# Moving x pairs to other PSUM banks, re-ordering query sums, and adding a third block of x on GpSimd in a fused attention and highway kernel

## The chip, the cores and the metric

The kernel runs on one core of one Trainium2 chip. Times are device microseconds (us) of that core. A kernel's time is the median of its runs; a profile is one execution, whose span is some 2 us shorter than the time of its run. The granted clock is the share of TensorE's full clock that the profile shows it was given.

Medians and ranges below are of all runs. A run over 1.5% above the fastest of its kernel counts as slow and is left out of the ratios, which are the mean time of one kernel's fast runs over that of the other's fast runs of the same rounds. The base of a ratio matters here: those of e1 to e3 come out at 133.45 us for the kernel before and those of e6 to e8 at 133.07, while all its fast runs on these chips average 132.62 and 132.28.

The engines are TensorE (PE), VectorE (DVE), ScalarE (ACT), GpSimd (POOL) and the queue that starts transfers (SP). In the timelines here each one's instructions follow the order in which the program issues them, and it waits where an input or a buffer is not ready.

## The reference, cut to what matters

```python
def _attn_ref(q, k, v):                      # 8 batches, 8 heads, 576 rows, 64 wide
    q_s = exp(q - max(q)); q_s = q_s / sum(q_s, axis=-1)
    k_s = exp(k - max(k)); k_s = k_s / sum(k_s, axis=2)
    kv = einsum('bhsd,bhse->bhde', k_s, v)
    return einsum('bhsd,bhde->bhse', q_s, kv)

def _moe_ref(x, w_h, w_t, b_t):              # x: 4608 x 512, from the attention
    H = maximum(x @ w_h, 0)
    T = 1 / (1 + exp(-(x @ w_t + b_t)))
    return T * H + (1 - T) * x               # = T * (H - x) + x
```

For each batch the kernel makes kv, then x, then the gates T and H. The last form of the result is the one it uses: g = T * (H - x) from DVE, plus x. That last plus x is what the third part of the change moves.

## The kernel before

The kernel's steps are placed by hand: `at(p, step)` puts a step at position p, and steps are issued in order of p, eight positions to a batch. So p decides what stands before what in each engine's queue. `E(f, ...)` only delays the call.

```python
    ps_ht = pool("ps_ht", 4, space=PSUM)     # the gates' banks
    ps_2 = pool("ps_2", 1, space=PSUM)       # one tile of two banks
    ps_1 = pool("ps_1", 1, space=PSUM)
    ps_nat = pool("ps_nat", 1, space=PSUM)
    # ... (cut)
    def x_pair(b, a, how, left=False, singles=False):
        # ... (cut: four x products; banks are two of ps_ht if singles, else the two of ps_2)
        copy = {"A": nc.scalar.copy, "V": nc.vector.tensor_copy}
        # ... (cut: "AV" copies the first bank on ACT and the second on DVE, "A" both on ACT)

    added = lambda g: (0, 1) if g < 3 else (0, 1, 2)

    def add_x(c, ob):                        # g += x for block ob of batch c, on GpSimd
        xv, gv = views(c)
        nc.gpsimd.tensor_add(gv(ob), gv(ob), xv(ob))

    def turn_block(t, k_, xs, us):           # transpose on PE; adds x there if xs is given
        dst = t[:, k_, :]
        if xs is not None:
            mm(dst, xs, ident, True, False)
        mm(dst, us, ident, xs is None, True)
    # ... (cut)
    # in out_tile(g, n): four blocks of the pair of batches 2g and 2g+1
            turn_block(t, k_,
                None if k_ in added(g) else xT[g][:, k_, n].rearrange("p b d -> p (b d)"),
                gT[g][:, k_, n].rearrange("p b d -> p (b d)"))
    # ... (cut)
    # placing, for pair g: the eight output tiles; and for chunk (batch) c the adds
            for i in range(8):
                at(16 * (g + 1) + 2 + 2 * i, E(out_tile, g, i))
    for c in range(2, B):
        for ob in added(c // 2):
            at(8 * c + 2 * ob + 2.5, E(add_x, c, ob))
    # placing, for batch b with p = 8 * (b - 1): exp of the queries, half sums, scale
            e0, e1, s0, s1, sc = {
                3: (-2.6, -1.6, -1.1, -0.1, 1),
                4: (-5.5, -4.5, -3.7, -2.7, -2.6),
            }.get(b, (-5, -4, -3.9, -2.9, -2.8))
            # ...
            at(p + s0, E(q_sums, b, 0))
            at(p + s1, E(q_sums, b, 1), E(q_recip, b))
            at(p + sc, E(q_scale_p, b, 0, 4), E(q_scale_p, b, 4, N9))   # on GpSimd
            s = p + {3: 0, 4: 0}.get(b, -0.5)
            at(s, E(exp_half, b, "k", 0), E(cast_v, b, 0))              # cast on GpSimd
            at(s + 0.9, E(cast_v, b, 1))
```

The softmax here doesn't subtract the row's maximum and nothing guards it: scores larger than these inputs give would overflow.

Of the kernel before, what the change touches and what calls it, by code (L numbers as in the profile page):

```python
# [9 lines left out]
FP32 = mybir.dt.float32  # L10
# [8 lines left out]
def kernel(  # L19
# [10 lines left out]
    nc = tc.nc  # L30
    B, H, S, D = q.shape
    P = 128
# [17 lines left out]
    eqp = pool("eqp", 2)  # L50
    small = pool("small", 2)
    qtp = pool("qtp", 2)
    xtp = pool("xtp", 3)
    gp = pool("gp", 2)
    mo = pool("mo", 3)
    ps_ht = pool("ps_ht", 4, space=PSUM)
# [102 lines left out]
    def two_banks(name, dt=FP32):  # L159
        return ps_2.tile([P, 2, 2048 // (4 if dt is FP32 else 2)], dt, tag="q2", name=name)  # L160

    single = lambda name: ps_1.tile([P, 512], FP32, tag="q1", name=name)
    nat_bank = lambda name, dt=FP32: ps_nat.tile(
        [P, 512 if dt is FP32 else 1024], dt, tag="nat", name=name
# [114 lines left out]
    def x_mm(dst, b, a, c, x, n0, n1):  # L279
        r = slice(64 * c, 64 * c + 64)  # L280
        mm(
            dst[64 * x : 64 * x + 64], kvn[b % 2][r, x, a, :],
            qsT[b][r, 2 * a + x, n0:n1, :].rearrange("p n d -> p (n d)"), True, True,
        )


    def x9_mm(t, b, c):
        for a in range(2):
            for x in range(2):
                x_mm(t[:, c, a, :], b, a, c, x, NM, N9)  # L290

    def x9_copy(b, t, c=slice(0, 2)):
        x9v = x9.rearrange("p (a c) b d -> p c a b d", c=2)
        nc.vector.tensor_copy(x9v[:, c, :, b, :], t)

    def x_left(b):
        for c in range(2):
            name = f"px_{b}_l{c}"
            t = single(name) if c == 0 else two_banks(name)[:, 0] if b == 1 else nat_bank(name)
            t = t[:, 0:128].rearrange("p (z a w) -> p z a w", z=1, a=2)  # L300
            for a in range(2):
                for x in range(2):
                    x_mm(t[:, 0, a, :], b, a, c, x, NM, N9)
            x9_copy(b, t, slice(c, c + 1))
# [2 lines left out]



    def x_pair(b, a, how, left=False, singles=False):  # L310
        g, b2 = b // 2, b % 2
        if a == 0 and b2 == 0:
            xT[g] = xtp.tile([P, 4, NM, 2, 64], FP16, tag="xT", name=f"xT_{g}")
        if left and a == 0:
            t9 = ps_1.tile([P, 512], FP32, tag="q1", name=f"px_{b}_l")
            x9t[b] = t9[:, 0:256].rearrange("p (c a w) -> p c a w", c=2, a=2)
        if singles:
            t = [
                ps_ht.tile([P, 512], FP32, tag="ht", name=f"px_{b}_{a}_{c}")
                for c in range(2)  # L320
            ]
        else:
            t2 = two_banks(f"px_{b}_{a}")
            t = [t2[:, c] for c in range(2)]
        if left and a == 0:
            x9_mm(x9t[b], b, 0)
        for c in range(2):
            for x in range(2):
                x_mm(t[c], b, a, c, x, 0, NM)
        if left and a == 1:  # L330
            x9_mm(x9t[b], b, 1)
        dst = xT[g][:, 2 * a : 2 * a + 2, :, b2, :]
        view = lambda t: t.rearrange("p (n d) -> p n d", d=64)
        copy = {"A": nc.scalar.copy, "V": nc.vector.tensor_copy}
        if len(how) == 1:
            copy[how](dst, t2.rearrange("p c (n d) -> p c n d", d=64))  # L336
        else:
            for c in range(2):
                copy[how[c]](dst[:, c], view(t[c]))  # L339
        if left and a == 1:  # L340
            x9_copy(b, x9t[b])
# [51 lines left out]
        )  # L393


    added = lambda g: (0, 1) if g < 3 else (0, 1, 2)

    def add_x(c, ob):
        xv, gv = views(c)
# [82 lines left out]
    def at(p, *fs):  # L482
        events.setdefault(p, []).extend(fs)

    E = lambda f, *a: (lambda: f(*a))

    for c in range(1, B + 2):
        for ob in range(4):
            p = 8 * c + 2 * ob
# [6 lines left out]
    for g in range(B // 2):  # L496
        p = 16 * (g + 1)
# [6 lines left out]
    p = 8 * B + 8  # L504
# [1 line left out]
    at(p + 4, E(tile9, 1, 4))  # L506
    at(p + 8, E(tile9, 2, 3), E(tile9, 3, 3), E(last9))

    at(8, E(cast_v_head, 2, 0, nc.gpsimd), E(q_scale_p, 2, 0, 4), E(q_scale_p, 2, 4, 8))
    at(8.2, E(x_left, 1))  # L510
    at(9, E(exp_half, 2, "k", 0))
    at(10, E(cast_v_head, 2, 1, nc.scalar), E(exp_half, 2, "k", 1))
    at(10.5, E(blend, 0, 3))
# [7 lines left out]
    for b in range(2, B):  # L521
        p = 8 * (b - 1)
        if b > 2:
            e0, e1, s0, s1, sc = {
                3: (-2.6, -1.6, -1.1, -0.1, 1),
                4: (-5.5, -4.5, -3.7, -2.7, -2.6),
            }.get(b, (-5, -4, -3.9, -2.9, -2.8))
            at(p + e0, E(exp_half, b, "q", 0))
            at(p + e1, E(exp_half, b, "q", 1))
            at(p + s0, E(q_sums, b, 0))  # L530
            at(p + s1, E(q_sums, b, 1), E(q_recip, b))
            at(p + sc, E(q_scale_p, b, 0, 4), E(q_scale_p, b, 4, N9))
            s = p + {3: 0, 4: 0}.get(b, -0.5)
            at(s, E(exp_half, b, "k", 0), E(cast_v, b, 0))
            at(s + 0.9, E(cast_v, b, 1))
            at(s + 1, E(exp_half, b, "k", 1))
        tr, kv, x = {
            2: ((5, 6, 6.9), (4, 6.2), (7, 7.5)),
            3: ((3.5, 4.9, 5.1), (4, 4), (5.9, 6.9)),
            4: ((2, 3, 4), (4.5, 4.5), (5.9, 6.9)),  # L540
        }.get(b, ((2, 3, 4), (4, 4), (5, 6)))
        for i in range(3):
            at(p + tr[i], E(q_trans, b, i))
        at(p + kv[0], E(kv_half, b, 0))
        at(p + kv[1], E(kv_half, b, 1), E(kv_norm, b))
        at(p + x[0], E(x_pair, b, 0, "A", b > 2))
        at(p + x[1], E(x_pair, b, 1, "AV" if b == 2 else "A", b > 2, b == 2))
        if b == 2:
            at(p + 7.6, E(x_left, 2))
    for b in range(4, B):  # L550
        at(8 * (b - 3), *[E(load, b, w) for w in "qkv"])

    for f in [
        E(warm_up, 24),
        E(exp_half, 0, "q", 0), E(q_sums, 0, 0),
        E(exp_half, 0, "q", 1), E(q_sums, 0, 1),
        E(q_recip, 0), E(q_scale_v, 0, 0, 4), E(q_scale_v, 0, 4, N9),
        E(exp_half, 0, "k", 0), E(cast_v, 0, 0),
        E(exp_half, 0, "k", 1), E(cast_v, 0, 1),
        E(q_trans, 0, 0), E(q_trans, 0, 1, lambda: two_banks("pq_0_1", FP16)[:, 0]), E(warm_up, 2), E(q_trans, 0, 2, lambda: nat_bank("pq_0_2", FP16)),  # L560
        E(warm_up, 6),
        E(kv_half, 0, 0), E(gate_bias), E(warm_up, 2), E(kv_half, 0, 1), E(kv_norm, 0),
        *[E(cast_weight, "t", k_, (nc.vector, nc.gpsimd)[k_ % 2]) for k_ in range(4)],
        E(warm_up, 4),
        E(x_pair, 0, 0, "AA"), E(warm_up, 2), E(x_pair, 0, 1, "AV", False, True), E(warm_up, 1), E(x_left, 0),
        E(exp_half, 1, "q", 0), E(q_sums_tree, 1, 0),
        E(exp_half, 1, "q", 1), E(q_sums_tree, 1, 1), E(q_recip, 1),
        *[f for k_ in range(4) for f in (E(less_one, k_), E(cast_weight, "h", k_, nc.scalar, 0.5))],
        E(q_scale_p, 1, 0, 4), E(q_scale_p, 1, 4, 8),
        E(gate, 0, 0), E(gate, 0, 1), E(gate, 0, 2, lambda: two_banks("pt_0_2")[:, 0]), E(warm_mid, 5),  # L570
        E(carry, 0, 0), E(blend, 0, 0), E(carry, 0, 1), E(exp_half, 1, "k", 0),
        E(gate, 0, 3, lambda: nat_bank("pt_0_3")), E(blend, 0, 1), E(carry, 0, 2),
        E(q_trans, 1, 0), E(blend, 0, 2), E(carry_products, 0, 3),
        E(exp_half, 1, "k", 1),
        *[E(cast_v_head, 1, c, (nc.scalar, nc.gpsimd, nc.gpsimd, nc.scalar)[c]) for c in range(4)],
        E(q_scale_p, 1, 8, N9),
        *[E(load, 2, w) for w in "qk"], E(load, 2, "v", [nc.sync, nc.sync]),
        *[E(load, 3, w) for w in "qkv"],
        E(q_trans, 1, 1), E(kv_half, 1, 0), E(kv_half, 1, 1), E(kv_norm, 1),
        E(q_trans, 1, 2), E(carry_diff, 0, 3), E(exp_half, 2, "q", 0),  # L580
        E(x_pair, 1, 0, "AV"), E(x_pair, 1, 1, "AV", False, True),
        E(q_sums_tree, 2, 0), E(exp_half, 2, "q", 1), E(q_sums_tree, 2, 1), E(q_recip, 2),
    ]:
        f()
    for p in sorted(events):
# [32 lines left out]
```

## Time and profile before

| | before |
|---|---|
| time, median of 3 (later 4 runs: 133.32) | 133.96 us (132.43 to 134.23) |
| span of the profiled execution | 130.2 us (its run took 132.09, clock 1.00) |
| TensorE busy | 114.8 us, 88% |
| GpSimd adds of x | 18, mean 1151 ns |
| transposes of x on PE (nat from xT) | 56, each some 57 ns of issue |

The prediction below shows most of the lines. These are the ones that parts 1 and 2 aim at, from the timelines of DVE and of PE (start, length, engine, line, operation, output and input, count; in brackets the idle time before it and what ended it). In the names, pq is a query transpose, px and px_l an x product, psk the key-value (kv) product, nat an output tile, eq the exp of the queries and g the blend:

```profile
31.79 1.29 DVE L339 CAST xT<-px 128x512 f16<-128x512 f32 x2 [0.86 <-ACT xT L339]
```

```profile
54.72 0.27 PE L68 MATMUL pq<-ident,eq 128*128 128x128 f16 x2 [1.20 <-DVE qsT L277]
55.51 0.22 PE L63 MATMUL px_l<-qsT,kvn 64*64 64x64 f16 x2 [0.52 <-DVE qsT L277]
...
67.44 0.22 PE L63 MATMUL px_l<-qsT,kvn 64*64 64x64 f16 x2 [0.51 <-DVE kvn L219]
```

DVE's copy of x waited for ACT's, though the two read different banks. PE waited for DVE's query copies (qsT) and for the normalized kv (kvn), because reduces stood ahead of them in DVE's queue.

### The profile page before, as it was taken

Reading aid. Unit: us, or ns where it says so; the run is one execution under the profiler, and the core shown is the slowest. Engines: PE = TensorE matmul, PEld = TensorE weight load, DVE = VectorE, ACT = ScalarE, POOL = GpSimd, SP = SyncE. Lnnn points to the kernel's source line nnn. Section 1 sums busy time; section 2 is a strip of 40 time slices with the busy share of each in tenths; the row PEclk is TensorE's granted clock in tenths of the full one; section 3 lists DMA queues with packets and bytes.
Section 4 is the critical chain, followed back from the end, with each engine's and each line's share of the span. In section 5 each row is a group of like instructions: output and inputs, shape, how many; then the busy total and the mean of one; then the engine's idle time right before and its main releaser. Section 6 shows DMA issues by size and latency. Waiting matters only on the chain.

```text
span 130.2 us, 3470 instructions
## 1 busy us (share of the span) xinstructions
PE 114.8 (88%) x1431; PEld 64.5 (50%) x1431; DVE 99.8 (77%) x183; ACT 92.3 (71%) x129; POOL 70.5 (54%) x64
## 2 busy tenths in 40 slices
PE   4999997984988798599989999999999999999940
PEld 2335442461435345355644664465566445689930
DVE  1297537796999997986899689988998657669960
ACT  3543059987898489277979988998994665576430
POOL 2004526790299999639935991799299703600000
PEclk9999999999999999999999999999999999999999
DMA  4999999999999999995999999993025007055874
GB/s 125 366 379 397 407 401 412 411 411 411 406 411 409 404 413 410 403 413 216 310 371 410 414 271 410 403 430 138 0 121 206 0 5 322 0 242 242 360 304 149
DMA packets 15847, 40.06 MB, mean 308 GB/s; under 512 B 724, under 2 KB 1240, under 8 KB 14808
## 3 DMA queue, kind: packets, MB, share of 16 engines
q1 hardware_dynamic: 15832, 39.85, 79.5%
q8 instruction: 11, 0.18, 0.5%
q14 instruction: 4, 0.03, 0.1%
HBM read 30.41 MB, written 9.44 MB: 306 GB/s over the span
## 4 chain that ended last, share of the span: by engine, by line
PE 47%; DMA 19%; DVE 14%; POOL 9%; SPq 3%; issue 2%; ACT 2%; DVEq 0%; POOLq 0%
DMA q<-in_q_dram 19%; PE pt L63 17%; PE ph L63 15%; PE nat L63 6%; POOL eq L259 3%; PE pq L68 3%; DVE dd L383 3%; POOL g L400 3%; DVE g L391 2%; PE px L63 2%; PE psk L63 2%; SPq L95 2%; DVE r L229 2%; POOL v L192 2%; DVE xT L339 1%
## 5 line engine op out<-in xcount | busy, mean ns | idle before, releaser
L259 POOL TENSOR_TENSOR eq<-eq,r 128x1024 f16<-128x1024 f16 (+2 forms) x16 | 29.7, 1876 | 14.8 <-DVE r L247 14.3
L63 PE MATMUL pt<-xT,w16t 128*128 128x512 f16 x128 | 33.7, 379 | 2.8 <-DVE dd L383 1.3
L63 PE MATMUL ph<-xT,w16h 128*128 128x512 f16 x128 | 33.3, 380 | 1.1 <-ACT w16h L115 0.7
L365 ACT ACTIVATE pt<-pt,bt 128x512 f32<-128x512 f32 (+1 forms) x40 | 24.7, 622 | 12.0 <-PE pt L63 11.2
L391 DVE SCALAR_TENSOR_TENSOR g<-pt,dd 128x512 f16<-128x512 f32 (+1 forms) x40 | 25.0, 628 | 3.1 <-DVE dd L383 0.5
L383 DVE SCALAR_TENSOR_TENSOR dd<-xT,ph 128x512 f16<-128x512 f16 x32 | 21.8, 682 | 6.7 <-PE ph L63 6.6
L400 POOL TENSOR_TENSOR g<-g,xT 128x512 f16<-128x512 f16 x18 | 20.5, 1151 | 7.6 <-DVE g L391 7.5
L63 PEld LDWEIGHTS <-w16t 128*128 128x128 f16 x160 | 14.6, 97 | 18.1 <-issue 5.6
L180 ACT ACTIVATE eq<-q 128x1152 f16<-128x1152 f32 x16 | 18.6, 1173 | 5.3 <-DMA q<-in_q_dram 5.3
L180 ACT ACTIVATE ek<-k 128x1152 f16<-128x1152 f32 x16 | 18.6, 1173 | 1.7 <-DMA k<-in_k_dram 1.7
L63 PEld LDWEIGHTS <-w16h 128*128 128x128 f16 x160 | 13.7, 98 | 11.3 <-ACT w16h L115 2.5
L229 DVE TENSOR_REDUCE r<-eq 128x18 f32<-128x1152 f16 x12 | 16.1, 1344 | 3.8 <-ACT eq L180 3.8
L192 POOL CAST v<-v 128x1152 f16<-128x1152 f32 x12 | 13.5, 1147 | 10.1 <-DMA v<-in_v_dram 10.1
L63 PE MATMUL nat<-ident,g 128*128 128x128 f16 x142 | 17.7, 219 | 0.5 <-DVE g L391 0.2
L63 PEld LDWEIGHTS <-g 128*128 128x128 f16 x144 | 13.7, 98 | 7.1 <-DVE g L391 1.4
L336 ACT CAST xT<-px 128x1024 f16<-128x1024 f32 x11 | 11.2, 1016 | 7.2 <-PE px L63 7.2
L440 ACT COPY o<-nat 128x512 f32<-128x512 f32 x26 | 15.6, 600 | 0.1
L68 PE MATMUL pq<-ident,eq 128*128 128x128 f16 x144 | 12.0, 219 | 2.8 <-DVE qsT L277 2.1
L63 PE MATMUL warm<-wide,ident 128*128 128x512 f16 x41 | 12.6, 456 | 1.8 <-DVE wide L152 1.8
L277 DVE COPY qsT<-pq 128x1024 f16<-128x1024 f16 (+1 forms) x24 | 13.2, 553 | 1.1 <-PE pq L68 0.6
L68 PEld LDWEIGHTS <-eq 128*128 128x128 f16 x144 | 9.3, 97 | 7.3 <-issue 3.3
L63 PE MATMUL nat<-ident,xT 128*128 128x128 f16 x56 | 9.7, 219 | 0.0
(52 smaller groups left out, 100.4 us busy)
## 6 DMA issues: line engine op xcount, KB each, us to landing
out_dram<-o SPq DMA_DIRECT2D x8, 1024.0 KB, 5.2
q<-in_q_dram SPq DMA_DIRECT2D x7, 1152.0 KB, 13.7
k<-in_k_dram SPq DMA_DIRECT2D x7, 1152.0 KB, 13.2
v<-in_v_dram SPq DMA_DIRECT2D x5, 1152.0 KB, 13.6
v<-in_v_dram SPq DMA_DIRECT2D x6, 576.0 KB, 11.7
q<-in_q_dram SPq DMA_DIRECT2D x2, 576.0 KB, 4.0
k<-in_k_dram SPq DMA_DIRECT2D x2, 576.0 KB, 7.1
w32t<-in_moe_w_t_dram SPq DMA_DIRECT2D x1, 1024.0 KB, 11.0
```

The lines of the kernel that those rows point to most:

```text
L63: mm = lambda o, l, r, st, sp: nc.tensor.matmul(o, l, r, start=st, stop=sp, skip_group_check=True)
L68: nc.tensor.matmul(o, i, ident, is_transpose=True, start=True, stop=True, skip_group_check=True,)
L180: nc.scalar.activation(dst[b][:, :, 2 * a : 2 * a + 2, :], in32[which][b][:, 2 * a : 2 * a + 2].rearrange("p c n d -> p n c d"), AF.Exp,)
L192: (eng or nc.gpsimd).tensor_copy(o, i)
L229: nc.vector.reduce_sum(qsum[b][:, :, h], eq[b][:, :, h, :], axis=AX.X)
L259: nc.gpsimd.tensor_mul(e, e, r.broadcast_to(list(e.shape)))
L277: nc.vector.tensor_copy(qsT[b][:, :, n0:n1, :], t[:, :, 0:w, :])
L365: nc.scalar.activation(ps, ps, AF.Tanh, bias=bt2[:, ob : ob + 1], scale=0.5)
L383: nc.vector.scalar_tensor_tensor(dd, xv(ob), -0.5, ps, op0=ALU.mult, op1=ALU.max)
L391: nc.vector.scalar_tensor_tensor(gv(ob), th, 1.0, dd, op0=ALU.add, op1=ALU.mult)
L400: nc.gpsimd.tensor_add(gv(ob), gv(ob), xv(ob))
L440: nc.scalar.copy(o, flat(t))
```

## The change

Three things are meant to help. The first x pairs go into separate tiles, so that the ACT and DVE copies need not wait for each other. Batch 4's (and 5's) sums go behind the query copies that PE is waiting for. GpSimd, half idle, adds a third of the four blocks of x for pairs 1 and 2 (the second and third pair; the prediction's "pairs 2 and 3"), which spares PE 16 transposes. In the text that follows, "pair 2" and "pair 3" are used as in the prediction.

```diff
+    ht_bank = lambda name: ps_ht.tile([P, 512], FP32, tag="ht", name=name)
+    one_of_two = lambda name: two_banks(name)[:, 0]
 ... (cut: x_left and x_pair take their banks from a list of homes)
-    added = lambda g: (0, 1) if g < 3 else (0, 1, 2)
+    added = lambda g: (0, 1) if g < 1 else (0, 1, 2)
 ...
-    at(8, E(cast_v_head, 2, 0, nc.gpsimd), E(q_scale_p, 2, 0, 4), E(q_scale_p, 2, 4, 8))
+    at(8, E(cast_v_head, 2, 0, nc.gpsimd))
+    at(9.05, E(q_sums_tree, 2, 1), E(q_recip, 2))
+    at(9.1, E(q_scale_p, 2, 0, 4), E(q_scale_p, 2, 4, 8))
     at(8.2, E(x_left, 1))
+    at(16.2, E(x_left, 2))
 ...
-                4: (-5.5, -4.5, -3.7, -2.7, -2.6),
+                4: (-5.5, -4.5, -2.8, -1.5, -1.4),
+                5: (-5, -4, -3.4, -2.7, -2.6),
             }.get(b, (-5, -4, -3.9, -2.9, -2.8))
 ...
-        at(p + x[1], E(x_pair, b, 1, "AV" if b == 2 else "A", b > 2, b == 2))
-        if b == 2:
-            at(p + 7.6, E(x_left, 2))
+        homes = (single, nat_bank) if b == 2 else None
+        at(p + x[1], E(x_pair, b, 1, "AV" if b == 2 else "A", b > 2, homes))
 ...
-        E(q_trans, 1, 2), E(carry_diff, 0, 3), E(exp_half, 2, "q", 0),
-        E(x_pair, 1, 0, "AV"), E(x_pair, 1, 1, "AV", False, True),
-        E(q_sums_tree, 2, 0), E(exp_half, 2, "q", 1), E(q_sums_tree, 2, 1), E(q_recip, 2),
+        E(q_trans, 1, 2), E(carry_diff, 0, 3),
+        E(x_pair, 1, 0, "AV", False, (ht_bank, ht_bank)),
+        E(x_pair, 1, 1, "AV", False, (ht_bank, one_of_two)),
+        E(exp_half, 2, "q", 0), E(q_sums_tree, 2, 0), E(exp_half, 2, "q", 1),
```

More of the change, by code (lines that the diff above doesn't have):

```diff
@@ L298, in x_left @@
             name = f"px_{b}_l{c}"
-            t = single(name) if c == 0 else two_banks(name)[:, 0] if b == 1 else nat_bank(name)
+            t = single(name) if c == 0 else one_of_two(name) if b > 0 else nat_bank(name)
             t = t[:, 0:128].rearrange("p (z a w) -> p z a w", z=1, a=2)
@@ L306, with x_pair @@
     x9t = {}
-    def x_pair(b, a, how, left=False, singles=False):
+    def x_pair(b, a, how, left=False, homes=None):
         g, b2 = b // 2, b % 2
@@ L316, in x_pair @@
             x9t[b] = t9[:, 0:256].rearrange("p (c a w) -> p c a w", c=2, a=2)
-        if singles:
-            t = [
-                ps_ht.tile([P, 512], FP32, tag="ht", name=f"px_{b}_{a}_{c}")
-                for c in range(2)
-            ]
+        if homes:
+            t = [home(f"px_{b}_{a}_{c}") for c, home in enumerate(homes)]
         else:
@@ L564 @@
         E(warm_up, 4),
-        E(x_pair, 0, 0, "AA"), E(warm_up, 2), E(x_pair, 0, 1, "AV", False, True), E(warm_up, 1), E(x_left, 0),
+        E(x_pair, 0, 0, "AA"), E(warm_up, 2), E(x_pair, 0, 1, "AV", False, (ht_bank, ht_bank)), E(warm_up, 1), E(x_left, 0),
         E(exp_half, 1, "q", 0), E(q_sums_tree, 1, 0),
```

## The prediction

> **What bounds the kernel now.** All times are microseconds of the profiled execution (span 130.2) unless said otherwise. I read the page's busy table first, then the chain that ended last, then the windows by stage, and last the timelines of TensorE (PE), VectorE (DVE) and GpSimd (POOL) side by side.
>
> ```profile
> PE 114.8 (88%) x1431; PEld 64.5 (50%) x1431; DVE 99.8 (77%) x183; ACT 92.3 (71%) x129; POOL 70.5 (54%) x64
> ```
>
> The averages say PE, with GpSimd half idle. Two windows show that the stages differ:
>
> ```profile
> 36.00:48.00 12.00, 9.95 (x141) 5.12 (x139) 11.62 (x23) 9.45 (x13) 11.94 (x11) 1.00 1.04 409
> ...
> 94.70:106.00 11.30, 11.27 (x163) 6.46 (x162) 8.67 (x16) 7.74 (x13) 8.73 (x7) 1.00 0.23 94
> ```
>
> Columns are stretch, length, then PE, PEld, DVE, ACT, POOL. Between 36 and 48 GpSimd has no gap (11.94 of 12) and PE has; later PE has no gap (11.27 of 11.30) and anything that makes PE wait goes straight to the end. The chain that ended last agrees: up to 37.9 it runs through ACT and DVE, then through GpSimd, then mostly along PE from 49.57 to 113.
>
> ```profile
> 37.90 1.89 POOL eq L259
> 39.79 0.61 POOL v L200
> 40.40 0.57 POOL eq L259
> 40.97 4.05 POOL g L400 x4
> 45.02 0.09 issue
> 45.10 0.02 POOLq L192
> 45.12 0.09 issue
> 45.21 0.02 POOLq L259
> 45.22 0.13 issue
> 45.35 2.24 POOL v L192 x2
> 47.61 1.91 POOL eq L259
> 49.52 0.05 issue
> 49.57 0.62 PE pq L68 x8
> ```
>
> The reader should see that the transposes of batch 3's queries (pq) start when the first scale of those queries ends. For the third part of the change the lines that matter are GpSimd's and PE's. First GpSimd:
>
> ```profile
> 69.83 4.19 POOL L259 TENSOR_TENSOR eq<-eq,r 128x1024 f16<-128x1024 f16 x2 [3.26 <-DVE r L247]
> 73.96 2.24 POOL L192 CAST v<-v 128x1152 f16<-128x1152 f32 x2
> ...
> 93.67 4.19 POOL L259 TENSOR_TENSOR eq<-eq,r 128x1024 f16<-128x1024 f16 x2 [2.74 <-DVE r L247]
> 97.81 2.24 POOL L192 CAST v<-v 128x1152 f16<-128x1152 f32 x2
> ```
>
> and the PE steps that will depend on them:
>
> ```profile
> 73.54 0.28 PE L63 MATMUL nat<-ident,g 128*128 128x128 f16 x2
> ...
> 88.49 0.78 PE L63 MATMUL psk<-v,ek 64*64 64x65 f16 x72
> ...
> 96.26 0.28 PE L63 MATMUL nat<-ident,g 128*128 128x128 f16 x2
> ```
>
> The lines at 73.54 and 96.26 are the first output tiles of the second and third pair of batches; 88.49 is batch 6's key-value product, which needs batch 6's value casts (on GpSimd until 88.66).
>
> **What the Trainium skill says.** (1) "GPSIMD Engine Reference", Engine selection, puts two-input elementwise work on GpSimd at about half VectorE's speed. The trace is harsher: the 128x512 f16 add takes 1.15 on GpSimd, a 128x576 f16 add takes 0.45 on DVE. (2) "PSUM — Partial Sum Buffer", Specifications, says ScalarE and VectorE can use PSUM in parallel if they do not meet in a bank. In the trace batch 1's first x pair lies in two banks of one tile, and DVE's copy still waited 0.86 for ACT's; so here the order is kept by tile, and separate tiles should remove it. (3) "TensorE: Matmul & The Clock Gate", Back-to-back issue gap, gives about 134 cycles at 2.4 GHz, 56 ns, for 128 columns; the trace has six such matmuls in 0.34, 57 ns each. (4) The same page, HAM oscillation, warns of PE idle gaps above about 3.4 us, after which the clock falls. Gaps here reach 1.2 and the granted clock stays 1.00; the gaps I predict stay below that figure.
>
> **Part 1, first batches' x pairs, and the order of batch 2's sums.** Before: ACT first does the exp of batch 2's queries (30.12 to 31.28), then its two x copies; DVE's two copies start at 31.79 and end at 33.08, and gate (1,0) needs all four. After: px is ready near 30.55, so ACT copies at 30.55 and 31.05, DVE at about 30.87 (behind a 0.6 difference) and 31.47; the last ends near 32.15. PE gains about 0.9 there. But the exp now ends near 32.7. The half sum then takes 1.2, to 34.0 (before: 33.08 to 34.27). The second half's sum and the reciprocal, which came straight after, now stand behind the x-left copies (0.34) and a difference (0.6): 34.0 + 0.34 + 0.6 + 1.2 + 0.38 gives 36.5 for the reciprocal, where it was 35.88. GpSimd's scale of batch 2 waits for it, so the packed GpSimd stretch moves from 36.03 to about 36.6. Everything of the chain above moves with it: batch 3's first scale ends at 50.1, pq at about 50.1. PE, ahead by 0.5 to 0.9, waits there about 1.7, where it waited 0.44. Moving batch 2's second pair off the gates' banks lets gate (2,0) start some 0.5 earlier, before the same wait. Net of part 1 at that point: +0.55.
>
> **Part 2, batch 4's sums behind batch 3's query copies.** Before, a 1.26 reduce (52.80) stands ahead of a query copy, and PE waits 1.20 and then 0.52. After, with all of part 1's 0.55 in it, the DVE order is key-value norm (ends 53.25), copy 0.6, difference 0.6 once its product is done at 54.05, small copy 0.25, and the x product px(3,0) starts near 55.0 instead of 55.51, the reduce following it. Batch 4's reciprocal slips from 57.1 to 58.4, so its scale ends 62.65 and its casts 64.9, just in time for PE. The same move for batch 5 puts batch 4's norm ahead of a reduce: px(4,0) near 66.2 instead of 67.44. PE now leads by 1.2. But batch 5's reciprocal moves little: norm ends 66.0, + reduce 1.26, + difference 0.6, + reduce 1.26, + 0.38 = 69.5, before 69.66.
>
> **Part 3, one more block added on GpSimd for pairs 2 and 3.** It removes 16 matmuls of 57 ns from PE (0.9 in all) and adds four adds of 1.15 to GpSimd (4.6). GpSimd has idle time for them, but runs in program order, and three fall badly. The add for chunk 3 (position 30.5) is issued after batch 5's scales (29.4) and before batch 5's casts (31.5); the one for chunk 5 (46.5) after batch 7's scales (45.2); the one for chunk 4 (38.5) between batch 6's scales and its casts. The first output tile of the pair needs the first and second of these.
> - Batch 5's reciprocal to the next query transposes: before 73.88 - 69.66 = 4.2, set by PE. After: 0.15 start + 4.15 scales + 1.15 add + 0.2 rest of the tile = 5.65. Cost 1.4 against the reciprocal; PE, which would reach the tile near 72.3, stands for 2 to 2.7 and loses its lead of 1.2.
> - Batch 6's reciprocal to the end of its key-value product: before 89.2 - 82.15 = 7.05. After: 0.15 + 4.15 + 1.15 + casts 2.2 + second half of the product 0.45 = 8.1. Cost 1.05.
> - Batch 7's reciprocal (93.5 before) to its query transposes: before 96.6 - 93.5 = 3.1. After again 5.65. Cost 2.55, a PE gap of about 2.6.
> Sum 5.0. Of the saved matmuls only those behind the last gap count fully, 7 x 0.057 = 0.4; those between gaps only lengthen the next wait. With the shift of batch 5's reciprocal (-0.15) the end moves by 5.0 - 0.4 - 0.15 = about +4.4. From 96.6 on PE has no gaps in which to win it back. I take +4.2, since gaps let DVE catch up a little.
>
> **Rivals.** (a) The change does what it intends: PE is the bound, 0.9 of matmuls goes, and 1.2 of lead from parts 1 and 2 survives: about -2, 132 us. For it: GpSimd is 54% busy and idles before every scale (3.26, 3.81, 2.74). Against: those idles end before the blend that the add needs, so the add cannot use them; the order on GpSimd decides. (b) The waits cost less because DVE reaches the reciprocals earlier: about +1.5, 135.5. For: DVE has 2 to 3 idle per batch late on. Against: each reciprocal is tied to its batch's norm and so to PE. (c) The gaps lower PE's clock or add to each other: +6, 140. Against: no gap above 3.4 is expected, and the clock held through 1.2.
>
> **Range and chances.** The median before is 133.96; +4.2 gives 138.1. Parts 1 and 2 are uncertain by 0.6, the three waits by about 0.5 each and the base by 0.8 (132.43 to 134.23): about 1.4 together, so 136.2 to 139.8 for eight in ten. Two per cent slower is 136.6, which lies one such error below the middle: slower 0.85, same 0.12. Faster needs the GpSimd order to be misread: 0.03.
>
> **What would show it.** PE timeline: two gaps of 2 to 3 at the first tile of pairs 2 and 3, ended by the GpSimd add, and one near 1 within batch 6's key-value product, ended by the cast. The chain of waits runs there through DVE's reciprocal, scales and an add, no longer along PE. In the first part: no DVE wait for ACT's x copy, batch 2's reciprocal near 36.5, pq of batch 3 near 50.1. Batch 3's px near 55.0 and batch 4's near 66.2 would confirm part 2. It is wrong if PE passes the first tile of pair 2 without a gap, or if pair 2's first tile comes before 73.

## The result, and the profile after

The changed kernel takes 139.06 us (138.59 to 139.6, 4 runs) against 133.32 (132.43 to 134.23, later 4 runs of the kernel before; 133.96 was the median of 3): ratio 1.0432, 95% interval 1.0332 to 1.0531. It is slower, inside the predicted range. The profiled span is 136.8, 6.6 more than before.

The page's head, its busy line, and the PE and clock lines of its 40 slices (each slice 3.4 us):

```profile
span 136.8 us, 3442 instructions
...
PE 116.5 (85%) x1415; PEld 64.7 (47%) x1415; DVE 100.0 (73%) x183; ACT 92.3 (68%) x129; POOL 74.2 (54%) x68
...
PEclk9999999999999999999999599999999999999999
```

PE has 16 matmuls fewer and yet is busy 1.7 us longer: busy time is no measure of work here. The single 5 in the clock line, in the slice that starts near 75, is why: in e9's profile below, without it, PE is busy 114.0.

The timeline of PE, all its waits over 0.3 from 44 on but one of 0.90 at 44.72 that both kernels have in much the same form (0.85 before):

```profile
50.38 0.62 PE L69 MATMUL pq<-ident,eq 128*128 128x128 f16 x8 [1.36 <-POOL eq L262]
55.30 0.22 PE L64 MATMUL px_l<-qsT,kvn 64*64 64x64 f16 x2 [0.77 <-DVE qsT L280]
75.59 0.25 PE L64 MATMUL nat<-ident,g 128*128 128x128 f16 x1 [2.48 <-POOL g L400]
92.19 0.48 PE L64 MATMUL psk<-v,ek 64*64 64x65 f16 x36 [0.32 <-POOL v L195]
93.28 0.48 PE L64 MATMUL psk<-v,ek 64*64 64x65 f16 x36 [0.61 <-POOL v L195]
103.50 0.23 PE L64 MATMUL nat<-ident,g 128*128 128x128 f16 x1 [2.53 <-POOL g L400]
```

The timeline of GpSimd around the first and the last of these gaps:

```profile
70.25 4.19 POOL L262 TENSOR_TENSOR eq<-eq,r 128x1024 f16<-128x1024 f16 x2 [2.70 <-DVE r L250]
74.39 1.14 POOL L400 TENSOR_TENSOR g<-g,xT 128x512 f16<-128x512 f16 x1
...
98.16 4.19 POOL L262 TENSOR_TENSOR eq<-eq,r 128x1024 f16<-128x1024 f16 x2 [2.71 <-DVE r L250]
102.30 1.14 POOL L400 TENSOR_TENSOR g<-g,xT 128x512 f16<-128x512 f16 x1
```

The add that the first output tile of the pair needs ends at 75.53 and at 103.44, and PE goes on 0.06 later. It was issued behind two scales of 4.15 in all, and these could not start before the reciprocal (the idle 2.70 that DVE ends).

The window behind the first gap (stretch, length, busy of PE, PEld, DVE, ACT, POOL with counts, then granted clock, DMA share and GB/s):

```profile
75.50:79.20 3.70, 3.61 (x24) 2.51 (x25) 1.24 (x2) 1.65 (x2) 3.32 (x4) 0.54 0.93 302
```

The clock stood at about half for this stretch. From the resumed tile to batch 5's kv product PE took 80.53 - 75.59 = 4.94; in a later run of the same kernel without the fall (e9 below) the same steps took 79.06 - 75.69 = 3.37. So one fall costs about 1.6 us.

Parts 1 and 2 did what they were for. DVE's copy of x starts without a wait, at 30.83 where it was 31.79, while ACT's first copy still runs (30.62 to 31.21; timeline of DVE):

```profile
30.83 1.28 DVE L339 CAST xT<-px 128x512 f16<-128x512 f32 x2
```

The waits of 1.20 and 0.52 became one of 0.77, and that of 0.51 at batch 4's x product is gone (66.74, before 67.44). So PE came to the first late tile 0.7 ahead of before (72.84 for 73.54) and lost 2.48 there.

### The profile page after: what moved, and what is told of

Same layout as the page of the kernel before. It is cut to its first block, busy times and chain, and to the rows that moved or that the text cites. A ratio compares the mean times of both kernels' runs of the same rounds, so it can differ in the third digit from the quotient of the medians.

```text
span 136.8 us, 3442 instructions
## 1 busy us (share of the span) xinstructions
PE 116.5 (85%) x1415; PEld 64.7 (47%) x1415; DVE 100.0 (73%) x183; ACT 92.3 (68%) x129; POOL 74.2 (54%) x68
## 4 chain that ended last, share of the span: by engine, by line
PE 33%; DVE 18%; POOL 18%; DMA 7%; issue 7%; SPq 7%; ACT 6%; DVEq 0%; POOLq 0%; ACTq 0%
PE ph L64 10%; PE pt L64 10%; POOL eq L262 9%; DMA w32h<-in_moe_w_h_dram 7%; POOL g L400 6%; DVE dd L383 5%; PE nat L64 4%; PE pq L69 4%; SPq L96 4%; DVE r L232 4%; PE psk L64 3%; POOL v L195 3%; DVE g L391 3%; SPq L111 3%; ACT xT L336 2%
## 5 line engine op out<-in xcount | busy, mean ns | idle before, releaser
L64 PE MATMUL ph<-xT,w16h 128*128 128x512 f16 x128 | 34.2, 388 | 1.3 <-ACT w16h L116 0.7
L400 POOL TENSOR_TENSOR g<-g,xT 128x512 f16<-128x512 f16 x22 | 25.1, 1153 | 12.4 <-DVE g L391 12.4
L64 PE MATMUL nat<-ident,g 128*128 128x128 f16 x142 | 17.2, 220 | 5.4 <-POOL g L400 5.0
L64 PEld LDWEIGHTS <-g 128*128 128x128 f16 x144 | 13.1, 98 | 12.2 <-POOL g L400 5.4
L69 PE MATMUL pq<-ident,eq 128*128 128x128 f16 x144 | 12.8, 229 | 3.1 <-POOL eq L262 2.2
L69 PEld LDWEIGHTS <-eq 128*128 128x128 f16 x144 | 9.8, 103 | 8.2 <-POOL eq L262 5.1
L64 PEld LDWEIGHTS <-ident 128*128 128x128 f16 x46 | 4.8, 112 | 8.2 <-issue 4.4
```

Source lines behind the costliest of these rows:

```text
L64: mm = lambda o, l, r, st, sp: nc.tensor.matmul(o, l, r, start=st, stop=sp, skip_group_check=True)
L69: nc.tensor.matmul(o, i, ident, is_transpose=True, start=True, stop=True, skip_group_check=True,)
```

## The experiments

All ten runs computed the right result. In each group (e1 to e4, e5 to e8, e9 and e10) the runs of the kernel before were taken on the same chip. By a rule that asks for 2% beyond the noise, the changed kernel, e2 and e3 were classed as slower, e4 and e5 as the same, and all others as unclear; the intervals of e1, e6, e7 and e8 exclude 1, but not a gain under 2%.

**e1: parts 1 and 2 without part 3.**

```diff
-    added = lambda g: (0, 1) if g < 1 else (0, 1, 2)
+    added = lambda g: (0, 1) if g < 3 else (0, 1, 2)
```

> The changed kernel with part 3 undone (only two of four blocks added on GpSimd for pairs 1 to 3). Theory: parts 1 and 2 are worth the lead that PE has in the changed kernel before its first gap (batch 4's x product at 66.74, 67.44 before: 0.7), and with no late add this lead reaches the end: about 132.6 us, ratio to before 0.995, no PE gap over 1 us after 56, granted clock 1.00. Rival: the later reciprocals of batches 2 and 4 cost of themselves and are part of the loss: 134 us or more.

Measured: 130.99 us (130.89 to 131.11) against 132.67, ratio 0.9816 (0.977 to 0.9863). No PE wait over 0.3 stands behind 55. The rival falls: parts 1 and 2 are no part of the loss. The gain is larger than the expected 0.7 us, if by less than the ratio says: against all fast runs of the kernel before on this chip it is 1.6 us. Of those 23 runs nine had a mean clock of 0.968 to 0.976, and eight of the nine the longest spans (131.5 to 132.9); none of e1's four runs had so low a clock. What lowered it is not known.

**e2: part 3 alone, on the kernel before.**

```diff
-    added = lambda g: (0, 1) if g < 3 else (0, 1, 2)
+    added = lambda g: (0, 1) if g < 1 else (0, 1, 2)
```

> The kernel before with part 3 alone. Theory: nearly the whole loss is here. PE gaps at the first output tile of pair 2 (about 1.5 us), in batch 6's key-value product (about 1) and at the first tile of pair 3 (about 2.6), each ended by a GpSimd instruction that stands behind the added adds; saved matmuls give back 0.4: +4.5, about 137.9 us, ratio 1.034; 1.5 more for each time the clock falls behind a gap. Rival: the loss needs the later reciprocals of parts 1 and 2: then under +2.5, below 136 us.

Measured: 138.76 us (138.32 to 140.92) against 132.67, ratio 1.0387 (1.0325 to 1.0449); the run of 140.92 is a slow one. The waits on PE's timeline came nearly as expected (about 1.5 and 2.6):

```profile
75.78 0.23 PE L63 MATMUL nat<-ident,g 128*128 128x128 f16 x1 [1.36 <-POOL g L400]
...
102.11 0.29 PE L63 MATMUL nat<-ident,g 128*128 128x128 f16 x1 [2.53 <-POOL g L400]
```

Between them stand 0.33 and 0.61 in batch 6's kv product. Part 3 by itself carries the loss. With e1 and the changed kernel this makes a small table of fast means: parts 1 and 2 alone 131.0, part 3 alone 138.6, all three 139.1 (138.3 when repeated in e9). The gain of the first two does not lessen the loss of the third. PE's lead only made its first wait longer (1.36 here, 2.48 there), for the late add let PE go on at nearly the same time in both (75.78 and 75.59).

**e3: dummy matmuls in the two long gaps.**

```diff
             for i in range(8):
+                if g > 0 and i == 0:
+                    at(p + 2, E(warm_mid, 10))
                 at(p + 2 + 2 * i, E(out_tile, g, i))
```

> The changed kernel with ten dummy matmuls (2.2 us) ahead of each of the two first output tiles, into a free bank, so that PE works through most of the two gaps; nothing else moves. Theory: behind the first gap the clock fell to half for 3.3 us (window 72 to 84: 0.86) and cost 1.5; with the gap filled the clock stays 1.00 and the end comes 1.5 earlier than in the changed kernel in runs with one fall, 3 in runs with two: 136.5 to 137.8 us, ratio to before near 1.03. Rival: the clock has nothing to do with the gap: within 0.4 of the changed kernel (139.06), mean clock still under 0.99.

Measured: 137.2 us (136.57 to 137.41) against 132.67, ratio 1.0273 (1.0218 to 1.0328). As the clock theory had it: useless work made the kernel faster than the changed kernel, whose eight runs (here and in e9) all took longer than e3's slowest (137.65 and more, against 137.41). In e3's profile PE's waits at the two tiles are 0.33 and 0.37, and the clock is 1.00 behind both (75.80 to 79.30 and 102.20 to 105.70). The tiles go on at 75.85 and 102.18, as in the changed kernel's run without a fall (75.69 and 102.03, e9), so what remains of the loss is the wait for GpSimd itself, filled or not.

**e4: the same four adds at other places on GpSimd.**

```diff
+            if ob < 2 or c > 5:
                 at(8 * c + 2 * ob + 2.5, E(add_x, c, ob))
+    at(8 * 2 + 9.5, E(add_x, 2, 2))       # behind batch 4's casts
+    at(8 * 4 + 8.45, E(add_x, 4, 2))      # behind batch 6's casts
 ...
+            if b in (5, 7):
+                at(p + sc, E(q_scale_p, b, 0, 4))
+                at(p - 1.9, E(add_x, b - 2, 2), E(q_scale_p, b, 4, N9))
+            else:
                 at(p + sc, E(q_scale_p, b, 0, 4), E(q_scale_p, b, 4, N9))
```

> The changed kernel with the four new adds put elsewhere on GpSimd: those for chunks 3 and 5 between the two scale instructions of the next batch, those for chunks 2 and 4 behind the value casts. Same work on every engine. Theory: the order on GpSimd is the cause; both long gaps and the wait in batch 6's product go, PE keeps the 0.7 of lead and saves 0.9 of matmuls: about 131.7 us, ratio 0.988. Rival: GpSimd has too little time for four more adds, whatever their place: gaps appear elsewhere, 134 us or more.

Measured: 133.21 us (131.96 to 135.6, 20 runs) against 132.67, ratio 1.0022 (0.9989 to 1.0054). Order is the main cause: the same work at other places takes 4% off. But the expected gain did not come, and the result lies between theory and rival: it is 1.9 us behind e1 (fast means 132.9 and 131.0, same chip), which has the lead and no third add. The adds now push the second scale behind the moment PE needs it:

```profile
75.84 0.62 PE L69 MATMUL pq<-ident,eq 128*128 128x128 f16 x8 [0.64 <-POOL eq L262]
...
99.55 0.62 PE L69 MATMUL pq<-ident,eq 128*128 128x128 f16 x8 [0.64 <-POOL eq L262]
```

With 0.20 and 0.24 at the two first tiles that is 1.72 of new waits for at most 0.9 of saved matmuls. Between a reciprocal and the casts there was no free place for an add on GpSimd, neither behind the scales (the changed kernel) nor between them (e4).

**e5 and e6: part 1 alone, part 2 alone.** e5 is e1 with the two changed rows of sum positions as before; e6 is the kernel before with those two rows as in the change:

```diff
-                4: (-5.5, -4.5, -3.7, -2.7, -2.6),
+                4: (-5.5, -4.5, -2.8, -1.5, -1.4),
+                5: (-5, -4, -3.4, -2.7, -2.6),
```

> The kernel before with part 1 alone (x pairs in other banks, second half of batch 2's sums behind a difference). Theory: in the changed kernel batch 3's query transposes come 20.2 us after batch 1's x product, 19.4 before, because batch 2's reciprocal is later and GpSimd has no gap; nothing gives it back: 0.5 to 1 us slower than before, ratio about 1.005, a wait of 1.3 us for the scale where it was 0.44. Rival: freeing DVE from ACT's copy is a gain by itself: 0.5 us or more faster.

> The kernel before with part 2 alone (sums of batches 4 and 5 behind the query copies and the norm). Theory: all of the gain of the first two parts is here: the waits of 1.20 and 0.52 at batch 3's last transposes shrink to about 0.8 in all, that of 0.51 at batch 4's x product goes: 1.0 and 0.5, so 131.2 us, ratio about 0.989, less if the runs of before with a mean clock of 0.97 (1.5 us longer) come from that pause. Rival: the gain of parts 1 and 2 together (ratio 0.982) needs the other banks: then under 0.7 us.

Measured, e5: 133.27 us (131.68 to 135.3, 20 runs) against 132.82, ratio 1.005 (1.0018 to 1.0083). e6: 131.01 us (130.89 to 131.1) against 132.82, ratio 0.9845 (0.9777 to 0.9912). Both as the theory had them: part 1 by itself is a small loss, part 2 brings the gain. (Beside part 2 the small loss does not show: e1 has 130.99 on another chip.) In e6 PE goes through the place that had two waits with one:

```profile
54.83 0.22 PE L63 MATMUL px_l<-qsT,kvn 64*64 64x64 f16 x2 [0.77 <-DVE qsT L277]
```

e5's profile is of its slowest run (135.3), so no difference is read from it. But it shows the expected wait for the scale (1.35) and, early on, a fall of the clock (PE's timeline, then the window):

```profile
22.54 3.87 PE L64 MATMUL ph<-xT,w16h 128*128 128x512 f16 x8 [1.31 <-ACT w16h L116]
...
24.00:27.40 3.40, 3.30 (x8) 1.16 (x9) 2.28 (x5) 2.82 (x5) 3.20 (x2) 0.50 1.04 412
```

This fall came 1.5 behind a wait of 1.31, in a kernel without any gap of 2.5.

**e7: parts 1 and 2, with batch 2's sums where they were.**

```diff
-    at(9.05, E(q_sums_tree, 2, 1), E(q_recip, 2))
-    at(9.1, E(q_scale_p, 2, 0, 4), E(q_scale_p, 2, 4, 8))
+    at(8.1, E(q_scale_p, 2, 0, 4), E(q_scale_p, 2, 4, 8))
 ...
         E(exp_half, 2, "q", 0), E(q_sums_tree, 2, 0), E(exp_half, 2, "q", 1),
+        E(q_sums_tree, 2, 1), E(q_recip, 2),
```

> Parts 1 and 2 without the move of batch 2's sums: banks changed, but both half sums and the reciprocal straight behind each other as before. Theory: the reciprocal comes 0.9 to 1.0 earlier than with parts 1 and 2 (no x-left copies and no difference before it), GpSimd starts its gapless stretch that much earlier, and PE's wait of 1.36 for batch 3's scale shrinks by it: 0.7 to 1 us faster than parts 1 and 2, about 130.2 us, ratio 0.976. Rival: the difference that now comes later holds the gates up by the same: within 0.3 us of parts 1 and 2.

Measured: 130.05 us (129.62 to 130.84) against 132.82, ratio 0.978 (0.9699 to 0.9861). The theory holds: part 1's loss was in the reciprocal that its re-ordering delayed, not in its banks. GpSimd's scale of batch 2 starts at 35.27 (36.91 in the changed kernel), and PE's wait for batch 3's scale is

```profile
49.43 0.62 PE L69 MATMUL pq<-ident,eq 128*128 128x128 f16 x8 [1.06 <-POOL eq L262]
```

where it was 1.36. In the profiles of e7 and e1, where batch 1's queries landed at the same time (their exp starts at 18.46 and 18.43), these transposes start 0.63 earlier (49.43 for 50.06) and the span is 0.7 shorter. The difference that now comes later makes PE wait 1.25 at 36; GpSimd, which started 1.64 earlier than in the changed kernel, stands 0.63 at 45.27, and whether the one causes the other is not shown. This version is the fastest measured: 1.0 us under e6 on the same chip with no run in common, and some 6% under the changed kernel; that it is 2% under the kernel before is unclear.

**e8: parts 1 and 2, a third add for six of eight tiles, behind the casts.**

```diff
+    def add_x_part(c, ob, n0):
+        xv, gv = views(c)
+        o, i = gv(ob)[:, n0:NM], xv(ob)[:, n0:NM]
+        nc.gpsimd.tensor_add(o, o, i)
 ...
-                None if k_ in added(g) else xT[g]...
+                None if k_ in added(g) or (k_ == 2 and n > 1 and g > 0) else xT[g]...
 ...
+    for c, pos in ((2, 25.5), (3, 32.45), (4, 40.45), (5, 48.45)):
+        at(pos, E(add_x_part, c, 2, 2))
```

> Parts 1 and 2, with part 3 cut down: the third block is added on GpSimd only for output tiles 2 to 7 of pairs 2 and 3, issued behind the next value casts, where nothing waits for it; tiles 0 and 1 keep their transposes of x. Theory: 12 matmuls of 57 ns go and no wait comes: 0.7 us faster than parts 1 and 2, about 130.3 us, ratio 0.977. Rival: a GpSimd that does more slows VectorE or makes the next scale late: no gain or a loss, 131 us or more.

Measured: 130.89 us (130.82 to 131.02) against 132.82, ratio 0.9838 (0.9756 to 0.9921). The theory's half about waits is right, PE has no wait over 0.3 behind 55.6; its half about the gain is not: 0.1 us of the expected 0.7. In the profiles, from batch 3's x product to the issue of the last store, e8 takes 125.60 - 55.54 = 70.06 and e1 125.38 - 54.99 = 70.39, so 0.3. The chain that ended last (start, length, engine and line) shows where some of the rest went. In e1 it stays on PE through this stretch; in e8 it leaves PE:

```profile
79.83 0.66 ACT pt L365
...
80.89 1.03 ACT xT L336
...
81.96 0.59 PE pt L64 x2
```

The next gate's matmuls wait for ACT's copy of x, so transposes saved just ahead of it are saved for nothing. What explains the difference between 0.3 in the profile and 0.1 in the medians is open; the landing of batch 1's queries differs by 0.8 between these two profiles (their exp starts at 18.43 in e1, 19.23 in e8).

**e9 and e10: the changed kernel again, and with the first gap alone filled.** e10 has e3's edit with `g == 1` for `g > 0`.

> The changed kernel once more, for a comparison with the next run on the same chip in the same rounds. Theory: each long gap (2.5 us) can be followed by a stretch at half clock that costs 1.5; runs have one or two of them (mean clock 0.988 or 0.973): 138.6 to 139.6 us, ratio about 1.043. Rival: the first result was a chip's own: ratio 1.03 or less.

> The changed kernel with the ten dummy matmuls ahead of pair 2's first output tile alone; the second gap stays 2.5 us. Theory: no fall at the first gap, a fall in some runs at the second: between the changed kernel and the one with both gaps filled, 137.2 to 138.8 us, about 1 us under the changed kernel; runs with a mean clock above 0.98 near 137.2, none at 0.973. Rival: clock falls come from the whole load and not from a gap: same mix of clocks as the changed kernel.

Measured, e9: 138.69 us (137.65 to 140.95) against 132.7, ratio 1.0479 (1.0413 to 1.0544). e10: 139.32 us (137.33 to 139.55) against 132.7, ratio 1.0478 (1.0342 to 1.0615). One run of each (140.95 and 139.55) is slow. The first result was not a chip's own. The expected 1 us between e9 and e10 did not come. Falls come in some runs and not in others: e9's profiled run (137.65, clock 0.998) had none, with the same two gaps of 2.48 and 2.53 on its timeline; three of e10's four runs had a mean clock of 0.986 or 0.987 and one, at 137.33, had 0.997. The windows behind the first and the second gap of e10's profile say where:

```profile
75.80:79.30 3.50, 3.37 (x37) 2.24 (x37) 2.37 (x4) 1.94 (x3) 3.36 (x4) 1.00 0.98 326
102.20:105.70 3.50, 3.44 (x25) 2.22 (x26) 1.64 (x3) 0.59 (x1) 3.29 (x4) 0.63 0.07 21
```

The filled gap has no fall behind it, the open one has. In e2 too the fall (0.58 from 102 to 106) came at the end of the gap of 2.53 and not at that of 1.36. So of six gaps of 2.5 that were profiled three had a fall and three had none. The falls of all four profiles that have one (the changed kernel, e2, e5, e10) lasted 3.4 to 3.5 at a clock of 0.50 or 0.51. The counts are too small for a rate, and e10 by itself does not refute that the mix of clocks is the same as e9's.

## Why the prediction was right

It said slower, 138.1 us, by way of three waits that GpSimd's order would put on PE. The runs bear out the mechanism: part 3 alone carries the loss (e2), the waits stand at the three places named, and other places for the same adds take the loss away (e4). Point by point, with the ends of the reciprocals as marks:

| stretch | before | predicted change | changed kernel | e9, without a fall |
|---|---|---|---|---|
| end of batch 5's reciprocal | 69.66 | -0.15 | 70.08 (+0.42) | 70.18 (+0.52) |
| from there to batch 6's reciprocal | 12.49 | +1.4 | 15.49 (+3.00) | 13.92 (+1.43) |
| to batch 7's reciprocal | 11.35 | +1.05 | 12.42 (+1.07) | 12.41 (+1.06) |
| to batch 7's query transposes | 3.10 | +2.55 | 5.69 (+2.59) | 5.70 (+2.60) |
| to the end | 33.60 | -0.4 | 33.12 (-0.48) | 33.59 (-0.01) |
| sum | 130.2 | +4.45 | +6.6 | +5.6 |

- The three waits were sized well. The sums of scale, add and cast taken from the profile of before are within 0.05 where the clock held.
- The clock was mis-sized. The prediction kept a fall in its rival (c), as not expected, since no gap would exceed 3.4 us. Falls came all the same: 1.6 us in the profiled run, at the first gap of 2.48. With the gaps filled (e3) the time fell by 1.2 to 2.0 us (fast means 137.1 against 138.3 and 139.1, on other chips), so these falls go with these gaps. That a gap is all it takes, or that it must be so long, is not shown: e5's fall came behind 1.31.
- Part 1's delay was mis-sized by a little: batch 2's reciprocal ended at 36.76 where 36.5 was predicted, batch 3's transposes started at 50.38 for 50.1. The 0.5 that the banks were to give gate (2,0) was 0.1 (44.72 for 44.83). With part 2's x products at 55.30 (predicted 55.0) and 66.74 (66.2) this puts batch 5's reciprocal 0.6 later than predicted.
- Part 2's gain and part 1's loss were given the right signs (e6 0.9845, e5 1.005), and that PE's lead would not survive the first gap was right.
- The 0.4 of saved matmuls behind the last gap was about 0.28, measured to the issue of the last store (29.78 before, 29.51 in the changed kernel, 29.50 in e9). The landing of that store took 3.6 to 4.1 and covers the difference in either direction.
- That the number fell inside the range is in part luck. The medians differ by 139.06 - 133.32 = 5.74, where 4.2 was predicted; the base was taken as 133.96, which four runs put at 133.32. With that base the same +4.2 would have given 137.5 and a range up to 139.2, with the result just inside. The profile it was worked out on was of a run of 132.09 at full clock.
- The 56 ns that the prediction cites for a transpose ("TensorE: Matmul & The Clock Gate", Back-to-back issue gap) hold on that page for a matmul by itself; for a stream in which each has its weight load, as here, it gives about 81 ns. The trace's 57 ns is what the sum rests on.

Two things stay open. Where the runs of the kernel before with a mean clock near 0.97 lose it was not caught in a profile; the 16 runs of e1, e6, e7 and e8, all with part 2, have none below 0.98. And what sets off a fall was not settled: why a gap of 2.5 is followed by one in one run and not in another, and why e5 had one without such a gap.

## What to carry to other kernels

An engine that is half idle is free only where its queue is free: before giving it more work, place the new instruction in its program order and ask which instruction behind it is waited for, and what the new one itself must wait for behind. A saved instruction on the busiest engine counts only where no other wait ends just after it, and a pause on TensorE can cost more than its length: here, in some runs, a clock fall worth 1.6 us followed a pause of 2.5. If several changes are made together, run each alone: here one was a gain of 1.0 to 1.5%, one a loss of 0.5% that a small re-ordering seems to turn into a gain, and one the whole loss.

## What the Trainium skill lacked or had wrong

- "TensorE: Matmul & The Clock Gate", HAM oscillation: it names idle gaps above about 3.4 us as the danger. Here gaps of 2.48 and 2.53 us were followed by a stretch at half clock (0.54 over 3.7 us, 1.6 us lost) in some runs and not in others, and in e5 one began 1.5 us behind a wait of 1.31 us. How short a pause can be and still be followed by a fall no page says.
- "GPSIMD Engine Reference", Engine selection: about half of VectorE's speed for two-input work. A f16 add of 512 elements took 1.15 us on GpSimd, one of 576 on VectorE 0.45 us: nearly three times as long per element.
- No page has it: with two banks of one PSUM tile, VectorE's copy still waited for ScalarE's (0.86 us); from two separate tiles the copies overlapped (ScalarE's from 30.62 to 31.21, VectorE's from 30.83). Whether the chip or the program's own bookkeeping of tiles kept the order is not shown.
